# A start time for waiting streams in a kernel's written-out plan

## The chip, the core and the metric

The kernel runs on one core of a Trainium2 chip. The core has TensorE (PE; its weight loads are shown apart as PEld), VectorE (DVE), ScalarE (ACT), GpSimd (POOL) and SyncE (SP), which here only issues DMAs. Each engine works through its instructions in order, and an instruction that waits for a semaphore holds everything behind it on that engine. The metric is the device time of one execution in microseconds.

## The reference

Eight batches of 576 tokens go through two blocks. The first is causal attention with 8 heads of 64, and a bias from a running sum:

```python
s_pos = np.maximum(s, 0.0)
cum = np.cumsum(s_pos, axis=-1)
bias = -(cum[:, :, :, None] - cum[:, :, None, :])
scores = np.where(causal, -1000000000.0, scores + np.minimum(bias, 0.0))
scores = scores - np.max(scores, axis=-1, keepdims=True)
```

followed by the exponential, the division by its sum and the product with v. The second mixes the result by a two-dimensional Fourier transform over tokens and channels (its real part is added), normalizes each token, and adds a two-layer MLP of width 512 to 2048 to 512 with a relu.

## The kernel before

**Attention** goes by pairs of heads, 32 in all (`NP`). For pair i, `load` (L441) brings q and k; `high` (L491) rounds both on ScalarE into the tile KQ and puts the bias rows beside them; `low` (L517) sends copies to the tiles Q1 and K1, where VectorE (L539) and GpSimd (L532) form what the rounding left out. `maxes` (L549) computes all scores once, row-wise, to find each row's maximum: ten matmuls (L564) into three banks, each reduced by VectorE (L569, L574) into `Mx`. The maxima are transposed (L586), copied by ScalarE (L590), and sent by a DMA from ScalarE's queue into one row of KQ (L593). `scores` (L598) then computes the scores a second time, transposed, with the maxima already inside the product (L615 and L616, one bank each), and ScalarE takes the exponential into the buffer P (L621). GpSimd clears the part above the diagonal (L628, L640). `av` (L645) multiplies with the values (L676) and ScalarE copies the result into the buffers `stage` (L686, L689); `recip` (L704) and `finish` (L727) divide by the sums. KQ, Q1 and K1 have three buffers, P four (one for each head), `stage` three.

**The Fourier transform** follows for each batch when its four pairs are finished: `folds` (L771, on VectorE, GpSimd and ScalarE), then `fourier` (L825, matmuls L843 to L890 and the additions L907). Its result goes to DRAM. The conversion of the MLP's weights runs beside attention.

**The MLP** normalizes tiles of 512 tokens. The first tiles start while attention's buffers are freed one after another in `tail` (L1350); `mlp` (L1274) and `evacuate` (L1217) handle two tiles in parts, and `fast_tile` (L317) the others.

**The order of the work** up to the first fast tile is not written by hand. Each of these functions is a stream: a Python generator that yields steps, and emits instructions between them. A step names an engine, a cost in microseconds, the events it depends on, and perhaps a ring, whose next buffer must be free. `wait(...)` is a step without an engine. `Flow` (L1488) is a planner: it keeps for each engine the time at which it comes free, computes for every stream the earliest time at which its step could start, and places the earliest. Among steps of the same engine that could start within 0.05 us of it, the one with the smallest due time is placed. A placed step moves its engine's time on, and its end plus a small lag becomes an event. Due times come from the table `PR`, in which `T` is the distance of two pairs. The planned times do not go into the program; the order in which steps are placed does, for each engine by itself, since the instructions are emitted in this order. On the chip, semaphores hold each instruction until its data are there.

One property of this planner is touched by the change. When a stream passes `wait(...)`, the planner knows the event's time, but the next step of the stream, and the streams it adds, start from the time at which their engine is free and from the events they name themselves. In `scores`, the blocks' first step names no event:

```python
_, hold = yield wait(ev("row", i), ev("low", i), ring=(ring("P", 4), 3))
...
e, hold = yield pe(2 * mm(n), ring=(ring("ps", 3), 1))
```

The row's event is set in `maxes` by the step of the issue (0.74 us) and 6.5 us after it:

```python
e = yield ("ACT", 0.74, (), None)
...
e = after(e, 6.5)
```

Of the kernel before, what the change touches and what calls it, by code (L numbers as in the profile page):

```python
# [29 lines left out]
N1 = 6  # L30
NW = 8
MARGIN = 1.5
PR = {'high': -1.41, 'hstep': 1.51, 'low': -1.79, 'lstep': 1.29, 'qs': -1.97, 'mx': -0.77, 'mxh': -2.63, 'mxc': 0.92, 'mt': 9.48, 'sc': -1.53, 'sch': 7.21, 'scs': 0.71, 'sel': 9.19, 'av': 8.0, 'avh': 10.43, 'avk': 5.44, 'rc': 2.01, 'fin': 8.67, 'fold': 4.28, 'fj': 1.4, 'fst': 0.85, 'fou': 7.17, 'gap': 5.72, 'fo2': 28.57, 'fo3': 31.26, 'gap2': 0.06, 'cv': 0.11, 'T': 16.03}
BACKLOG = 4.0


# [6 lines left out]
def fused_kernel(ctx, tc, qkT, vA, sP, wP, tabD, tabS, corr, out):  # L43
# [375 lines left out]

    T = PR['T']  # L420
    L = NP - 1
# [176 lines left out]
    def scores(i):  # L598
        st = sts[i]
        qy, ky, q1, k1 = st["qy"], st["ky"], st["q1"], st["k1"]  # L600
        st["P"], st["Phold"] = [], []
        scored = Last(ev("scored", i), 12)
        for h in range(2):
            _, hold = yield wait(ev("row", i), ev("low", i), ring=(ring("P", 4), 3))
            P = attp.tile([128, PW], F32, tag="P", name="P", bufs=4)
            st["P"].append(P)
            st["Phold"].append(hold)
            diag = Last(Event(), 5)

            def one(h, c, a, n, P, diag):  # L610
                nk, q0, nq, qk = CH[c]
                ksl = slice(128 * c, 128 * c + 128)
                e, hold = yield pe(2 * mm(n), ring=(ring("ps", 3), 1))
                p = bank("ps")
                nc.tensor.matmul(p[:, :n], ky[:, h, ksl], qy[:, h, a:a + n], start=True, stop=False)  # L615
                nc.tensor.matmul(p[:, :n], k1[:, h, ksl], q1[:, h, a:a + n], start=False, stop=True)  # L616
                scored.add(e)
                lo = max(a, qk)
                o = POFF[c] + lo - qk
                e = yield act(a + n - lo, e)  # L620
                nc.scalar.activation(P[:, o:o + a + n - lo], p[:, lo - a:n], AF.Exp, scale=0.125)  # L621
                hold.add(e)
                if c < 4:
                    diag.add(e)
                else:
                    e = yield pool_(64, e)
                    d5 = P[:, POFF[4]:POFF[4] + 64]
                    nc.gpsimd.affine_select(out=d5, in_=d5, pattern=[[1, 64]], compare_op=ALU.is_ge, fill=0.0, base=0, channel_multiplier=-1)  # L628
                    ev("P5", i, h).set(e)

            x = 0
            for c, (nk, q0, nq, qk) in enumerate(CH):
                for a, n in [(0, 256), (256, 320)] if c == 0 else [(q0, nq)]:
                    flow.add(one(h, c, a, n, P, diag), T * i + PR['sc'] + PR['sch'] * h + PR['scs'] * x)
                    x += 1

            def select(P, diag, h):
                e = yield ("POOL", 0.8, (diag.event,), None)
                d4 = bass.AP(tensor=P.tensor, offset=P.offset, ap=[list(P.ap[0]), [576, 4], [1, 128]])
                nc.gpsimd.affine_select(out=d4, in_=d4, pattern=[[0, 4], [1, 128]], compare_op=ALU.is_ge, fill=0.0, base=0, channel_multiplier=-1)  # L640
                ev("P4", i, h).set(e)

            flow.add(select(P, diag, h), T * i + PR['sch'] * h + PR['sel'])

    def av(i):  # L645
        st = sts[i]
# [298 lines left out]
    def pair(i):  # L945


        yield from load(i) if i >= 3 else ()
        flow.add(high(i), T * (i + PR['high']), PR['hstep'])
        yield wait(ev("q", i, 1))  # L950
        flow.add(low(i), T * (i + PR['low']), PR['lstep'])
        flow.add(maxes(i), T * (i - 1) + PR['mt'])
        yield wait(ev("row", i), ev("low", i), *(at(("scored", i - 1)) if i else ()))
        flow.add(scores(i), T * i - 1.0)
        yield wait(ev("va", i), ev("P4", i, 0))
        flow.add(av(i), T * i + 7.0)
        yield wait(ev("sums", i))
        flow.add(recip(i), T * (i + 1) + PR['rc'])
        yield wait(ev("rb", i), *(at(("out", i - 1)) if i else ()))
        flow.add(finish(i), T * (i + 1) + PR['fin'])  # L960

    def pairs():
        for i in range(NP):
            if i >= 3:
                yield wait(ev("scored", i - 3))
            flow.add(pair(i), T * (i - 3))

    def batches():
# [248 lines left out]
    def evacuate(n, j, acc, e):  # L1217


        p, t0, f, _, _ = todo[n]  # L1220
        _, r = LN[t0]
        if p:
            e, ohold = yield ("DVE", 0.65, (e, ev("norm", t0)), (ring("oo", 2), 1))
            o = op.tile([128, TOK], F32, tag="o", name="o", bufs=2)
        else:
            e, khold = yield ("DVE", 0.65, (e, ev("norm", t0)), (ring("lt", 4), 1))
            o = lnp.tile([128, TOK], F32, tag="t", name="o", bufs=4)
        nc.vector.tensor_mul(o, r, acc[j])
        ev("acc", p, j).set(e)
        if not p:  # L1230
            got, hold = yield dma(256, *at(*(("part", last_of[1], j) for j in range(4))), ring=(ring("oo", 2), 1))
            w = op.tile([128, TOK], F32, tag="o", name="o", bufs=2)
            nc.sync.dma_start(out=w, in_=uD[j, :, t0:t0 + TOK])
            e = yield pool_(512, e, got)
            nc.gpsimd.tensor_add(o, w, o)
            hold.add(e)
            kept[j] = (o, khold)
            ev("part", n, j).set(e)
            return
        if p == 1:  # L1240
            yield wait(ev("fetched", j))
            w, hold = ws[j]
            e = yield pool_(512, e, ev("fetched", j))
            nc.gpsimd.tensor_add(w, w, o)
            ohold.add(e)
            if j == 3:
                e = yield dma(256, e)
                nc.sync.dma_start(out=uD[j, :, t0:t0 + TOK], in_=w)
                hold.add(e)
            ev("part", n, j).set(e)  # L1250
            return
        ev("rhold", t0).hold.add(e)
        yield wait(ev("part", last_of[p - 2], j))
        w, khold = kept.pop(j)
        e = yield pool_(512, e, ev("part", last_of[p - 2], j))
        nc.gpsimd.tensor_add(w, w, o)
        ohold.add(e)
        e = yield dma(256, e)
        nc.sync.dma_start(out=out[j, :, t0:t0 + TOK], in_=w)
        khold.add(e)  # L1260
        ev("part", n, j).set(e)
# [226 lines left out]
class Flow:  # L1488
# [4 lines left out]
    def __init__(self):  # L1493
        self.free = dict.fromkeys(("PE", "ACT", "DVE", "POOL", "SP"), 0.0)
        self.wire = 0.0
        self.live = []

    def add(self, gen, due, step=0.0):
        self.send([gen, due, step, None], None)

    def send(self, s, got):
        new = s[3] is None
        try:
            s[3] = s[0].send(got)
        except StopIteration:
            if not new:
                self.live.remove(s)
            return
        s[1] += s[2]
        if new:  # L1510
            self.live.append(s)

    def start(self, step):
        engine, _, deps, ring = step
        t = self.free[engine] if engine else 0.0
        if ring:
            deps = (*deps, ring[0].next())
        late = MARGIN if engine == "SP" else 0.0
        for d in deps:
            if d.t is None:  # L1520
                return None
            t = max(t, d.t + late)
        return t

    def run(self, *goals):
        while any(g.t is None for g in goals):
            ready = [(t, s) for s in self.live for t in (self.start(s[3]),) if t is not None]
            if not ready:
                raise RuntimeError("the plan is stuck: " + str([(s[0].__qualname__.split(".")[-1], s[1]) for s in self.live]))
            t, s = min(ready, key=lambda x: (x[1][3][0] is not None, x[0]))  # L1530
            engine = s[3][0]
            t, s = min(((u, v) for u, v in ready if v[3][0] == engine and u <= t + 0.05), key=lambda x: x[1][1])
            self.place(s, t)

    def place(self, s, t):
# [5 lines left out]
        elif engine:  # L1541
            self.free[engine] = t + cost
            e = Event(t + cost + self.LAG[engine])
        else:
            e = Event(t)
        self.send(s, (e, ring[0].take(ring[1])) if ring else e)

# [177 lines left out]
```

## Time and profile before

| | |
|---|---|
| time, median of 3 runs | 1433.82 us (1433.74 to 1438.87) |
| profiled execution | 1436.77 us, its span 1435.0 us |
| mean granted TensorE clock | 0.958 |
| TensorE busy | 1284.5 us, 90% of the span, 7582 matmuls |
| VectorE busy | 828.3 us, 58% |
| ScalarE busy | 632.1 us, 44% |
| GpSimd busy | 511.6 us, 36% |

Busy shares are averages over stages with different limits: attention and the Fourier transform up to about 600 us, a short change-over, then the MLP. Names like `ps<-KQ` give the tile written and a tile read, and L615 is line 615 of the kernel before. A wait is told as the instruction that waits, and the one that released it. The granted clock is the share of TensorE's full clock. Matmuls are pipelined, so that the lengths of single ones overlap.

### The profile page before, as it was taken

The numbers are of one execution on the slowest core, as the hardware profiler recorded it, in microseconds if no ns is written. First come the engines' busy times: TensorE is split into PE (matmuls) and PEld (weight loads), VectorE is DVE, ScalarE is ACT, GpSimd is POOL, SyncE is SP. The second block draws the span as 40 slices with busy tenths as digits, with TensorE's granted clock in tenths as the row PEclk, the third lists the DMA queues.
The fourth block names the chain that finished last, engine by engine and source line by source line (L and its number), as shares of the span: only waits on it lengthen the run. The fifth ranks groups of instructions, "written<-read, shape, count | busy, mean of one in ns | idle before, by whom it ended". The sixth has DMA issues, their size and how long they took to land.

```text
span 1435.0 us, 21558 instructions
## 1 busy us (share of the span) xinstructions
PE 1284.5 (90%) x7582; PEld 1129.2 (79%) x7582; DVE 828.3 (58%) x1784; ACT 632.1 (44%) x1452; POOL 511.6 (36%) x499
## 2 busy tenths in 40 slices
PE   4688777877888998889999989999999999999998
PEld 3576666766777777778878878888888888898887
DVE  5366747565766675678496568535445444554423
ACT  3566655644656565554253324333233333323321
POOL 6244446453546462573477244110211102021100
PEclk9899988978999999999999999999999999999999
DMA  8546456544545564464586233444435344342433
GB/s 219 156 120 158 121 169 183 153 125 121 155 127 157 135 173 105 128 221 142 195 257 207 98 129 103 142 138 127 167 100 177 106 147 148 125 169 89 140 125 118
DMA packets 119687, 210.79 MB, mean 147 GB/s; under 512 B 15801, under 2 KB 37753, under 8 KB 119579
## 3 DMA queue, kind: packets, MB, share of 16 engines
q1 hardware_dynamic: 116939, 206.19, 46.8%
q0 software_dynamic: 1712, 2.53, 0.8%
q8 instruction: 60, 0.98, 0.3%
q10 hardware_dynamic: 928, 0.69, 0.2%
q14 instruction: 48, 0.39, 0.1%
HBM read 153.69 MB, written 31.72 MB: 129 GB/s over the span
## 4 chain that ended last, share of the span: by engine, by line
PE 65%; DVE 12%; DMA 10%; ACT 5%; issue 4%; POOL 3%; SPq 1%; ACTq 0%; DVEq 0%; POOLq 0%
PE b L343 17%; DMA KQ<-mt 7%; PE pav L676 7%; PE acc L255 7%; PE acc L254 7%; PE acc L256 7%; PE pm L564 4%; PE ps L615 4%; PE ps L616 3%; PE h L1316 3%; PE pz L843 2%; DVE trash L574 2%; ACT P L621 1%; DVE K L539 1%; PE acc L1298 1%
## 5 line engine op out<-in xcount | busy, mean ns | idle before, releaser
L676 PE MATMUL pav<-P,va 128*128 128x320 f32 (+4 forms) x896 | 218.6, 383 | 9.2 <-ACT stage L686 3.3
L615 PE MATMUL ps<-KQ 128*128 128x256 f32 (+2 forms) x384 | 136.0, 362 | 89.3 <-DMA KQ<-mt 79.2
L676 PEld LDWEIGHTS pav<-P,va 128*128 128x128 f32 x896 | 167.0, 203 | 45.0 <-issue 8.9
L574 DVE CUSTOM_DVE_ANT_0 trash<-pm,amask 128x256 bf16<-128x256 f32 (+3 forms) x256 | 124.5, 486 | 129.8 <-PE pm L564 111.1
L621 ACT ACTIVATE P<-ps 128x320 f32<-128x320 f32 (+4 forms) x384 | 138.5, 394 | 132.0 <-PE ps L616 125.4
L255 PE MATMUL acc<-zh,w2l 128*128 128x512 f32 x452 | 179.6, 397 | 0.0
L254 PE MATMUL acc<-zh,w2h 128*128 128x512 f32 x452 | 179.2, 397 | 0.0
L256 PE MATMUL acc<-zl,w2h 128*128 128x512 f32 x452 | 177.4, 392 | 0.1
L301 POOL TENSOR_TENSOR w<-w,o 128x512 f32<-128x512 f32 x28 | 37.8, 1360 | 348.3 <-DVE o L297 309.2
L615 PEld LDWEIGHTS ps<-KQ 128*128 128x128 f32 x384 | 82.6, 215 | 100.0 <-issue 46.8
L564 PE MATMUL pm<-KQ 128*128 128x256 f32 (+3 forms) x384 | 133.3, 395 | 22.7 <-ACT KQ L509 11.8
L616 PE MATMUL ps<-Q,K 128*128 128x256 f32 (+2 forms) x384 | 125.9, 334 | 0.0
L335 ACT ACTIVATE zh<-cs 128x256 fp32r<-128x256 f32 x112 | 58.8, 525 | 142.7 <-DVE cs L355 88.5
L564 PEld LDWEIGHTS pm<-KQ 128*128 128x128 f32 x384 | 79.8, 220 | 38.4 <-DVE Mx L574 18.3
L336 DVE SCALAR_TENSOR_TENSOR zl<-cs,zh 128x256 fp32r<-128x256 f32 x112 | 66.3, 592 | 69.2 <-ACT zh L335 69.2
L343 PEld LDWEIGHTS b<-bh,wh 128*128 128x128 f32 x448 | 84.0, 188 | 25.1 <-DVE cs L355 5.7
L640 POOL TENSOR_SCALAR_AFFINE_SELECT P<-P 128x512 f32<-128x512 f32 x64 | 44.5, 695 | 160.4 <-ACT P L621 158.8
L256 PEld LDWEIGHTS acc<-zl,w2h 128*128 128x128 f32 x452 | 85.3, 189 | 19.8 <-DVE zl L336 0.6
L532 POOL TENSOR_TENSOR Q<-qk,Q 64x576 fp32r<-64x576 f32 x64 | 94.1, 1488 | 18.6 <-DMA Q<-KQ 15.0
L343 PE MATMUL b<-bh,wh 128*128 128x256 f32 x448 | 89.0, 280 | 4.4 <-DVE cs L355 4.4
L343 PE MATMUL b<-bh,wl 128*128 128x256 f32 x448 | 89.1, 280 | 0.0
L343 PE MATMUL b<-bl,wh 128*128 128x256 f32 x448 | 89.1, 280 | 0.0
(203 smaller groups left out, 2939.6 us busy)
## 6 DMA issues: line engine op xcount, KB each, us to landing
w2h<-w2D SPq DMA_DIRECT2D x128, 256.0 KB
w2l<-w2D SPq DMA_DIRECT2D x128, 256.0 KB
qk<-in_qkT_dram SPq DMA_DIRECT2D x32, 576.0 KB
raw<-in_wP_dram SPq DMA_DIRECT2D x32, 512.0 KB
va<-in_vA_dram SPq DMA_DIRECT2D x32, 480.0 KB
u<-uD SPq DMA_DIRECT2D x10, 1024.0 KB
Q<-KQ SPq DMA_DIRECT2D x32, 288.0 KB
K<-KQ SPq DMA_DIRECT2D x32, 288.0 KB
```

What stands on the lines that cost most here:

```text
L254: nc.tensor.matmul(acc[j], a[:, cs], y, start=first, stop=False)
L255: nc.tensor.matmul(acc[j], b[:, cs], y, start=False, stop=False)
L256: nc.tensor.matmul(acc[j], a[:, cs], z, start=False, stop=final)
L336: nc.vector.scalar_tensor_tensor(out=y[1][:, at], in0=src, scalar=0.0, in1=y[0][:, at].bitcast(F32), op0=ALU.max, op1=ALU.subtract)
L343: nc.tensor.matmul(p[:, 0:256], a[:, j * 128:(j + 1) * 128], b[:, j], start=start and i == 0, stop=i == 5, skip_group_check=not start)
L532: nc.gpsimd.tensor_sub(q1[64:128, h], qk[0:64, h], q1[0:64, h].bitcast(F32))
L564: nc.tensor.matmul(p[:, :n], qy[:, h, 128 * c:128 * c + 128], ky[:, h, k0:k0 + n], start=True, stop=True)
L574: nc.vector.tensor_tensor_reduce(out=trash[:, :n], in0=p[:, :n], in1=amask[:, m0:m0 + n], scale=1.0, scalar=first if x else NEG, op0=ALU.a ...
L615: nc.tensor.matmul(p[:, :n], ky[:, h, ksl], qy[:, h, a:a + n], start=True, stop=False)
L616: nc.tensor.matmul(p[:, :n], k1[:, h, ksl], q1[:, h, a:a + n], start=False, stop=True)
L621: nc.scalar.activation(P[:, o:o + a + n - lo], p[:, lo - a:n], AF.Exp, scale=0.125)
L676: nc.tensor.matmul(p[:, a - lo:n], va[:, c, vs], P[:, o:o + w], start=c == 0, stop=c == cs[-1])
```

## The change

A stream gets a fifth field, its floor. Passing a `wait` sets the floor to the time at which the wait ends in the plan; steps are placed from the floor on, and a stream that is added takes over the floor of the one that adds it. With this rule some waits would hold back streams that begin early, so they are moved: pairs begin when the scores four pairs back are done, not three; a pair no longer waits for its casts before `low` and `maxes` are added (their steps name these events themselves); and the scores of a pair follow an event "begun" of the pair before, set when its scores have been added and carrying the time of its row, in place of "scored", which is the end of its last block. In `evacuate`, a step names the event at which its pool opens. Most of the due times in `PR` change.

```diff
-PR = {'high': -1.41, 'hstep': 1.51, 'low': -1.79, 'lstep': 1.29, 'qs': -1.97, 'mx': -0.77, 'mxh': -2.63, 'mxc': 0.92, 'mt': 9.48, 'sc': -1.53, 'sch': 7.21, 'scs': 0.71, 'sel': 9.19, 'av': 8.0, 'avh': 10.43, 'avk': 5.44, 'rc': 2.01, 'fin': 8.67, 'fold': 4.28, 'fj': 1.4, 'fst': 0.85, 'fou': 7.17, 'gap': 5.72, 'fo2': 28.57, 'fo3': 31.26, 'gap2': 0.06, 'cv': 0.11, 'T': 16.03}
+PR = {'high': -1.4, 'hstep': 0.87, 'low': -1.9, 'lstep': 1.25, 'qs': -2.56, 'mx': -0.77, 'mxh': -2.85, 'mxc': 0.92, 'mt': 9.41, 'sc': -1.53, 'sch': 6.02, 'scs': 0.73, 'sel': 8.63, 'av': 9.99, 'avh': 15.59, 'avk': 4.5, 'rc': 2.01, 'fin': 26.62, 'fold': 4.29, 'fj': 1.4, 'fst': 1.56, 'fou': 7.67, 'gap': 4.39, 'fo2': 28.57, 'fo3': 32.04, 'gap2': 2.76, 'cv': 1.58, 'T': 16.07}
...
             flow.add(select(P, diag, h), T * i + PR['sch'] * h + PR['sel'])
+        ev("begun", i).set(ev("row", i))
...
         flow.add(high(i), T * (i + PR['high']), PR['hstep'])
-        yield wait(ev("q", i, 1))
         flow.add(low(i), T * (i + PR['low']), PR['lstep'])
         flow.add(maxes(i), T * (i - 1) + PR['mt'])
-        yield wait(ev("row", i), ev("low", i), *(at(("scored", i - 1)) if i else ()))
+        yield wait(ev("row", i), ev("low", i), *(at(("begun", i - 1)) if i else ()))
...
-            if i >= 3:
-                yield wait(ev("scored", i - 3))
+            if i >= 4:
+                yield wait(ev("scored", i - 4))
...
-            e, ohold = yield ("DVE", 0.65, (e, ev("norm", t0)), (ring("oo", 2), 1))
+            e, ohold = yield ("DVE", 0.65, (e, ev("norm", t0), ev("opened")), (ring("oo", 2), 1))
...
+        self.floor = 0.0
 
     def add(self, gen, due, step=0.0):
-        self.send([gen, due, step, None], None)
+        self.send([gen, due, step, None, self.floor], None)
 
     def send(self, s, got):
         new = s[3] is None
+        outer, self.floor = self.floor, s[4]
         try:
             s[3] = s[0].send(got)
...
+        finally:
+            self.floor = outer
...
-    def start(self, step):
-        engine, _, deps, ring = step
-        t = self.free[engine] if engine else 0.0
+    def start(self, s):
+        engine, _, deps, ring = s[3]
+        t = max(self.free[engine], s[4]) if engine else s[4]
...
         else:
+            s[4] = t
             e = Event(t)
```

More of the change, by code (lines that the diff above doesn't have):

```diff
@@ L1526, in run @@
         while any(g.t is None for g in goals):
-            ready = [(t, s) for s in self.live for t in (self.start(s[3]),) if t is not None]
+            ready = [(t, s) for s in self.live for t in (self.start(s),) if t is not None]
             if not ready:
```

## The prediction

> **What bounds the kernel now.** I read the page first, then busy time by stage, then the waits of TensorE in the attention stage, then its order of work around one wait, then the granted clock behind such waits.
>
> Busy time, from the first scores matmul to the last (first row), in the change-over (second) and in the MLP stage; columns: stretch, length, busy time and instructions of each engine, granted clock, DMA share, GB/s:
>
> ```profile
> 28.20:593.50 565.30, 460.35 (x2448) 396.50 (x2449) 354.06 (x997) 329.70 (x810) 270.38 (x287) 0.91 0.53 144
> ...
> 593.50:650.00 56.50, 51.37 (x320) 45.71 (x321) 42.65 (x62) 33.41 (x71) 38.02 (x32) 0.97 0.61 207
> 650.00:1435.00 785.00, 764.57 (x4799) 682.43 (x4797) 414.46 (x680) 261.48 (x561) 184.04 (x149) 0.99 0.43 142
> ```
>
> The MLP stage is TensorE's: busy 764.57 of 785.00 us at clock 0.99. The plan's rule cannot win much there: its matmul streams wait for the same events as their steps already name. Attention is different. TensorE is idle 565.30 - 460.35 = 104.95 us and its clock is 0.91, while the next busiest engine, VectorE, works 354.06 us, 63%. So nothing there is full; TensorE's in-order queue waits. What for, in the same stretch (us in total, times, longest):
>
> ```profile
> PE ps L615 <- DMA KQ<-mt: 79.2, 26, 6.4
> PE pm L564 <- DVE Mx L574: 8.0, 11, 2.2
> PE ps L615 <- DMA sums<-stage: 3.5, 1, 3.5
> PE pav L676 <- ACT stage L686: 3.3, 3, 2.9
> ```
>
> Three quarters of it, 79.2 of 104.95 us, is one wait: the scores of a pair (L615) stand for the row of maxima that ScalarE's queue sends into KQ (L593). All other causes share 25.8 us. TensorE's order at one such place (start, length, idle before and its releaser at the end):
>
> ```profile
> 435.73 0.27 PE L586 MATMUL pmt<-ident,Mx 128*10 128x128 f32 x1
> 435.76 0.36 PE L564 MATMUL pm<-KQ 128*128 128x256 f32 x1
> 435.96 1.78 PE L676 MATMUL pav<-P,va 128*128 128x320 f32 x6
> 437.34 0.53 PE L615 MATMUL ps<-KQ 128*128 128x256 f32 x1
> ...
> 437.82 0.65 PE L676 MATMUL pav<-P,va 128*128 128x192 f32 x4
> 438.28 0.54 PE L564 MATMUL pm<-KQ 128*128 128x256 f32 x2
> 442.30 0.55 PE L615 MATMUL ps<-KQ 128*128 128x256 f32 x1 [3.48 <-DMA KQ<-mt]
> ```
>
> The transpose of the maxima (L586) starts at 435.73, and the scores that need the row start at 442.30: 6.57 us. The order has only some 3.1 us of other work between them, so 3.48 us are idle. Later the same distance is filled:
>
> ```profile
> 485.58 0.27 PE L586 MATMUL pmt<-ident,Mx 128*10 128x128 f32 x1
> ...
> 490.99 0.54 PE L564 MATMUL pm<-KQ 128*128 128x256 f32 x2
> 491.36 0.28 PE L615 MATMUL ps<-KQ 128*128 128x256 f32 x1
> ```
>
> Here Fourier matmuls of another stream lie between, 5.78 us pass, and there is no wait. So the wait is one of order, not of capacity.
>
> **The change part by part.** *The floor.* In the old plan a score block's first step lists only its bank as a dependence; the wait for the row stands in the stream around it and moves nothing in time. So the plan places the block as soon as TensorE is free, though its own code counts 0.74 us for the issue and 6.5 us for the landing. With the floor, the block starts in the plan at the row's event, and TensorE's empty time before it goes to whatever is ready. Is the plan's distance right on the chip? ScalarE around the same place, and the same wait on the chain that ended last (third row: start, length):
>
> ```profile
> 436.40 0.24 ACT L590 CAST mt<-pmt 10x128 fp32r<-10x128 f32 x1
> 436.67 0.73 ACTq L593 DMA_DIRECT2D KQ<-mt  x1
> ...
> 436.67 5.50 DMA KQ<-mt
> 20.81 7.34 DMA KQ<-mt
> ```
>
> From the issue's start the row takes 5.50 us here and at most 7.34 (the startup), against 0.74 + 6.5 = 7.24 in the plan: the reserve covers it. Is there enough to fill it? TensorE's groups in the stretch (count, busy us, mean ns, idle before):
>
> ```profile
> L676 PE MATMUL pav<-P,va 128*128 128x256 f32 x864 | 210.2, 381 | 6.9 <-ACT stage L686 3.3 <-POOL P L628 1.9 <-issue 1.7
> L564 PE MATMUL pm<-KQ 128*128 128x512 f32 (+1 forms) x368 | 125.6, 386 | 9.9 <-DVE Mx L574 8.0 <-ACT KQ L513 0.4 <-issue 0.4
> ```
>
> Over 31 pairs the attention-times-values matmuls (L676) alone are 210.2 / 31 = 6.8 us a pair, with Fourier work beside them; all of pair i-1's can run while pair i's row travels. The first wait, 6.4 us at the first pair, has nothing to fill it and stays. For the others I leave half a microsecond in each of 30 pairs, 15 us, since ScalarE's queue ahead of L590 can make the row later than planned. Removed: 79.2 - 6.4 - 15 = 58 us. Bounds: 72.8 (all but the first) and 36 (half of that: fillers that are not ready either).
>
> *The clock.* Five microseconds from the end of a wait, first and last of those with a low clock, and between them one behind a short wait:
>
> ```profile
> 67.95:72.95 5.00, 5.00 (x19) 4.81 (x20) 1.89 (x7) 2.64 (x7) 0.00 (x0) 0.50 0.55 177
> ...
> 407.59:412.59 5.00, 5.00 (x18) 4.13 (x19) 1.94 (x8) 2.60 (x6) 2.34 (x2) 0.66 0.01 1
> 424.72:429.72 5.00, 5.00 (x35) 4.91 (x36) 2.18 (x13) 3.62 (x8) 1.34 (x2) 1.00 0.22 67
> ...
> 541.80:546.80 5.00, 5.00 (x17) 4.68 (x18) 2.78 (x11) 2.12 (x5) 0.42 (x1) 0.50 0.00 0
> 407.59 0.44 PE L615 MATMUL ps<-KQ 128*128 128x256 f32 x1 [2.75 <-DMA KQ<-mt]
> 424.72 0.36 PE L615 MATMUL ps<-KQ 128*128 128x256 f32 x1 [1.48 <-DMA KQ<-mt]
> ```
>
> Behind a wait of 2.75 us the clock is 0.66 and 18 matmuls run in 5 us; behind 1.48 us it is 1.00 and 35 run. Of the 17 stretches with a low clock all lie between 0.50 and 0.70; their shortfall adds up to 33 us of work at full clock (bound from the whole stretch: 460.35 x 0.09 = 41). A wait that only becomes shorter also wins this back. I take three quarters, 25 us; bounds 8 and 33.
>
> [...]
>
> *What comes instead.* The same work in a shorter stretch meets the other limits more often: VectorE's 354.06 us and ScalarE's 329.70 us would be 70% and 65% of some 505 us. The other waits, 25.8 us now, grow; I take 20 us more, bounds 0 and 26 (doubled).
>
> *Scores behind "begun" instead of "scored".* The next pair's scores need no longer follow the last of the pair before; the order of the P buffers is kept by the ring. With the floor this removes a bar that the floor would have made real. Likewise the pairs now start four back, and the wait on the casts goes: the buffers' own releases (qk, KQ) still hold the loads and casts, and every step there names its data. Taken as 0 on the path: they keep what the old plan did. Uncovered, a load later by a pair would be a new wait of the kind above, a rival below.
>
> *Other streams under the floor.* Fourier's second products and the folds, too, get their honest start; their waits on TensorE's list above are small. The change-over has only 56.50 - 51.37 = 5.1 us idle, so 0, bounds +5 and -10 (weight loads placed later while TensorE has no Fourier work left). The added dependence of the accumulator's evacuation on "opened" says only that its buffer exists: 0, covered by the MLP's first six hidden blocks.
>
> *The refitted numbers.* They set who goes first among ready steps, and cost no instruction. Two move far: the second head's values matmuls come 7.15 us later against their pair (9.99 + 15.59 after 8.00 + 10.43), which makes them the filler behind the next pairs' scores, and the finishing multiplications 18 us later (a rival). No instruction is added or removed on any engine.
>
> **Sum.** 58 + 25 - 20 = 63 us. The profiled execution took 1436.77 us (its span is 1435.0), so 1374; the median of the runs, 1433.82, is 2.95 below the profiled one: **1371 us**. Ends of the terms: 72.8 + 33 + 5 = 111 gives 1323; 36 + 8 - 26 = 18 gives 1416 (the change-over's -10 would make it 1426).
>
> **The rivals.**
>
> *The wait moves to VectorE.* With the row's wait filled by maxima blocks (L564), TensorE is three banks away from VectorE, which needs for them (rows by line, same stretch):
>
> ```profile
> L574 DVE CUSTOM_DVE_ANT_0 trash<-pm,amask 128x512 bf16<-128x512 f32 (+1 forms) x244 | 119.0, 488 | 127.1 <-PE pm L564 109.7 <-DVE Mx L574 0.5
> L574 DVE CUSTOM_DVE_ANT_0 trash<-pm,amask,M 128x320 bf16<-128x320 f32 x62 | 33.8, 545 | 21.0 <-PE pm L564 17.9 <-DVE M L569 0.2
> ```
>
> That is (119.0 + 33.8) / 31 = 4.9 us a pair against 125.6 / 31 = 4.1 us of busy matmul. For it: PE already waits for Mx 11 times. Against: VectorE itself waits 127 us for these matmuls, so it has room. Price: 45 instead of 20 us of new waits, each short enough to leave the clock alone: 58 + 25 - 45 = 38, 1396 us.
>
> *The change does not do what it says.* The old due times may already give the order that the new rule gives, and what is late on the chip is late for reasons outside the plan. For it: 7.24 us are counted correctly already. Against: the 3.1 us of filler at 435.73. Then the 79.2 us stay: 1430 us, give or take 6.
>
> *Slower: the finish holds ScalarE.* The finishing multiplications (L738, L742) free the stage buffers, three of them, that ScalarE's copies L686 and L689 write. By due times a finish lay 48.1 + 8.0 - (16.03 + 8.67) = 31.4 us ahead of the copy that reuses its buffer; now it is 48.2 + 9.99 - (16.07 + 26.62) = 15.5. If GpSimd runs later than that, the copy waits, and behind it in ScalarE's queue the exponentials, the casts and L590 with the next row: TensorE then waits for the row again. L689's waits show it once so far:
>
> ```profile
>   POOL xa L738: 4.1, 1
> ```
>
> At 4.1 us in three of five of 31 pairs it is 76 us, and the clock stays low: 58 - 76 = -18, so 1452 us; it decides from every second pair on (64 against 58). Against: GpSimd works 270.38 of 565.30 us.
>
> **How the numbers follow.** The forecast 0.58 (its own range 1323 to 1416), VectorE's wait 0.19, no effect 0.10, slower 0.13. About half a per cent, 7 us, is what a measurement of this kernel can tell from no change. Faster by more: 0.58 + 0.19, and a little of "no effect", 0.78. Within: 0.09. Slower: 0.13. For the range I leave out the lowest end, which needs every term at its best (some 0.05), and the slower case, and keep no effect: 1336 to 1436.
>
> **What would show it.** Right: the wait of L615 for the row falls from 79.2 to near 21 us; the granted clock in attention rises from 0.91 to 0.96 or more; L676 stands between L586 and the next L615; the last scores come some 60 us earlier than 593.5, and the 785 us behind them stay. The forecast is wrong if the row's wait stays over 50 us, if VectorE's Mx or ScalarE's stage takes over 40 us of TensorE, or if the change-over loses what attention wins.

## The result, and the profile after

The changed kernel takes **1363.18 us** (median of 4 runs, 1360.81 to 1364.03) beside 1435.68 for the kernel before: a ratio of **0.949, interval 0.9466 to 0.9515**. The forecast was 1371, in a range of 1336 to 1436. The profiled execution took 1363.77 us with a span of 1362.1.

The page of the kernel after, its head and the TensorE rows of the 40 slices:

```profile
span 1362.1 us, 21528 instructions
...
PE 1272.7 (93%) x7582; PEld 1112.4 (82%) x7582; DVE 831.1 (61%) x1784; ACT 625.5 (46%) x1452; POOL 511.8 (38%) x499
...
PE   5898889998989897999899899999999999999998
...
PEclk9999998999999899999999999999999999999999
```

The matmuls are the same 7582, and the other engines' busy times are within about 1% of what they were. TensorE's attention slices, mostly sevens and eights before, are now mostly eights and nines. Its busy time falls from 1284.5 to 1272.7 us for the same matmuls, while its mean granted clock rises from 0.958 to 0.975. Two stretches tell where the time went: from the first score block to the last, and from there to the end. The last score block before starts at 602.3 us; the prediction ended its stretch at 593.5, a little early. Before:

```profile
28.20:602.30 574.10, 469.15 (x2506) 404.55 (x2507) 358.71 (x1009) 335.73 (x826) 275.39 (x294) 0.91 0.52 143
```

and after, where the last two rows together are the rest (the columns are those of the prediction's first fence):

```profile
28.10:525.50 497.40, 450.52 (x2479) 380.18 (x2480) 355.87 (x994) 328.16 (x823) 278.26 (x294) 0.96 0.62 168
525.50:650.00 124.50, 114.69 (x723) 103.42 (x722) 86.87 (x127) 54.93 (x110) 63.45 (x51) 0.96 0.54 184
650.00:1362.10 712.10, 694.94 (x4357) 621.85 (x4355) 367.11 (x604) 234.84 (x510) 151.38 (x124) 0.99 0.42 139
```

The scores end after 497.40 in place of 574.10 us: 76.7 us won. The rest is 1362.1 - 525.5 = 836.6 us where it was 1435.0 - 602.3 = 832.7: 3.9 us given back. Inside the first stretch TensorE's idle time falls from 104.95 to 46.88 us (58.1 won), and its busy time from 469.15 to 450.52 (18.6 won), with the clock up from 0.91 to 0.96. Not all of the 18.6 us is shorter work: the stretch holds 27 matmuls fewer. The row ahead of it, from 0 to 28.1 us, has 12.59 us of busy TensorE in place of 8.19, and the rest has 809.63 in place of 807.14. So 4.4 us of work (8 matmuls) moved ahead and some 2.5 us (17 matmuls) behind, and 11.7 us is what the same matmuls take less over the whole kernel. What TensorE waits for in that stretch of the kernel after:

```profile
PE pm L564 <- DVE Mx L574: 26.6, 33, 3.8
PE ps L615 <- ACT P L621: 7.6, 8, 1.8
PE pz L844 <- DVE zs L852: 2.3, 1, 2.3
PE pmt L586 <- DVE Mx L574: 2.0, 3, 1.4
```

The row of maxima, 79.2 us in 26 waits before, is not in the list any more. The longest entry is now the maxima blocks' own wait for VectorE, 26.6 us in place of 8.0. In the view of the issue L593, the waits for the row that are left:

```profile
  PEld ps L615: 0.3, 1
```

And TensorE's order behind a transpose of maxima, in the kernel after:

```profile
299.82 0.28 PE L586 MATMUL pmt<-ident,Mx 128*10 128x128 f32 x1
...
300.06 0.28 PE L615 MATMUL ps<-KQ 128*128 128x256 f32 x1
...
300.88 2.92 PE L677 MATMUL pav<-P,va 128*128 128x256 f32 x14
...
309.38 3.03 PE L677 MATMUL pav<-P,va 128*128 128x256 f32 x14
...
312.83 1.36 PE L880 MATMUL py<-scos,zc 97*128 97x290 f32 x9
...
315.79 0.27 PE L586 MATMUL pmt<-ident,Mx 128*10 128x128 f32 x1
```

Between two transposes lie 16 us in which TensorE's list shows no idle time at all: score blocks of two pairs, maxima, both values products, and Fourier matmuls. The score block at 300.06 belongs to an earlier pair, for the row of this transpose is issued only at 300.42 (L593). So the row's way is filled with score blocks of earlier pairs as well as with values products.

### The profile page after: what moved, and what is told of

Read it like the earlier page. It is cut to its first block, busy times and chain, and to the rows that moved or that the text cites. A ratio compares the mean times of both kernels' runs of the same rounds, so it can differ in the third digit from the quotient of the medians.

```text
span 1362.1 us, 21528 instructions
## 1 busy us (share of the span) xinstructions
PE 1272.7 (93%) x7582; PEld 1112.4 (82%) x7582; DVE 831.1 (61%) x1784; ACT 625.5 (46%) x1452; POOL 511.8 (38%) x499
## 4 chain that ended last, share of the span: by engine, by line
PE 69%; DVE 15%; issue 5%; DMA 4%; POOL 3%; ACT 2%; SPq 1%; DVEq 0%; ACTq 0%; POOLq 0%
PE b L343 18%; PE pav L677 9%; PE acc L255 7%; PE acc L254 7%; PE acc L256 7%; PE h L1316 5%; DVE trash L574 3%; PE pm L564 3%; PE ps L615 3%; PE ps L616 2%; DVE K L539 2%; PE pz L844 2%; PE acc L1297 1%; PE acc L1298 1%; PE acc L1296 1%
## 5 line engine op out<-in xcount | busy, mean ns | idle before, releaser
L677 PE MATMUL pav<-P,va 128*128 128x320 f32 (+4 forms) x896 | 211.8, 378 | 1.1 <-POOL P L640 0.9
L677 PEld LDWEIGHTS pav<-P,va 128*128 128x128 f32 x896 | 163.5, 201 | 37.1 <-issue 6.1
L564 PE MATMUL pm<-KQ 128*128 128x256 f32 (+3 forms) x384 | 124.2, 381 | 45.6 <-DVE Mx L574 27.5
L621 ACT ACTIVATE P<-ps 128x320 f32<-128x320 f32 (+4 forms) x384 | 131.3, 394 | 47.3 <-PE ps L616 43.4
L615 PE MATMUL ps<-KQ 128*128 128x256 f32 (+2 forms) x384 | 125.9, 340 | 9.2 <-ACT P L621 7.6
L564 PEld LDWEIGHTS pm<-KQ 128*128 128x128 f32 x384 | 71.7, 200 | 71.5 <-DVE Mx L574 47.7
L616 PE MATMUL ps<-Q,K 128*128 128x256 f32 (+2 forms) x384 | 114.7, 308 | 0.0
L532 POOL TENSOR_TENSOR Q<-qk,Q 64x576 fp32r<-64x576 f32 x64 | 98.8, 1563 | 30.2 <-DMA Q<-KQ 15.2
L336 DVE SCALAR_TENSOR_TENSOR zl<-cs,zh 128x256 fp32r<-128x256 f32 x112 | 65.4, 584 | 69.3 <-ACT zh L335 69.3
L615 PEld LDWEIGHTS ps<-KQ 128*128 128x128 f32 x384 | 73.9, 192 | 17.8 <-ACT P L621 11.1
L255 PEld LDWEIGHTS acc<-zh,w2l 128*128 128x128 f32 x452 | 85.8, 190 | 2.5
```

The lines of the kernel that those rows point to most:

```text
L255: nc.tensor.matmul(acc[j], b[:, cs], y, start=False, stop=False)
L532: nc.gpsimd.tensor_sub(q1[64:128, h], qk[0:64, h], q1[0:64, h].bitcast(F32))
L564: nc.tensor.matmul(p[:, :n], qy[:, h, 128 * c:128 * c + 128], ky[:, h, k0:k0 + n], start=True, stop=True)
L677: nc.tensor.matmul(p[:, a - lo:n], va[:, c, vs], P[:, o:o + w], start=c == 0, stop=c == cs[-1])
```

## The experiments

The theory was that of the prediction: the plan put score blocks ahead of a row that it knew to be on its way, the floor stops that, and a TensorE that stands less keeps more of its clock (in the prediction's rows 0.66 behind a wait of 2.75 us, 1.00 behind one of 1.48). The rivals: the refitted due times make the gain; or the wait hides another; or the clock wins nothing. All times below are medians, ratios are against the kernel before, run beside each kernel.

**The rule with the due times of before.** The edit to the changed kernel is one line:

```diff
-PR = {'high': -1.4, 'hstep': 0.87, ... 'T': 16.07}
+PR = {'high': -1.41, 'hstep': 1.51, ... 'T': 16.03}
```

> The floor and the moved waits of the change, with the due times of before. Theory (the rule puts other work where TensorE stood for the row of maxima): the row's wait at L615 falls from 79.2 to under 15 us, the attention clock rises from 0.91 to 0.96 or more, and the time is 1375 to 1400 us. Rival (the refitted due times make the gain): the row's wait stays above 50 us or another wait of that size takes its place, 1420 us or more.

Measured: 1385.99 us, ratio 0.9663 (0.9633 to 0.9693). As the theory has it: the wait for the row is gone from the list, and the stretch of the scores is

```profile
28.40:541.30 512.90, 459.00 (x2484) 384.12 (x2485) 356.49 (x993) 328.99 (x824) 272.96 (x293) 0.94 0.59 161
```

so 61 us shorter than before; the clock, 0.94, rose less than the expected 0.96.

**The due times in the planner of before.**

```diff
-PR = {'high': -1.41, 'hstep': 1.51, ... 'T': 16.03}
+PR = {'high': -1.4, 'hstep': 0.87, ... 'T': 16.07}
```

> The refitted due times alone, in the planner of before. Theory: the plan still places score blocks ahead of their row, the row's wait stays above 50 us, and the time is 1415 to 1450 us. Rival (the due times make the gain): the row's wait is under 25 us and the time 1385 us or less.

Measured: 1438.15 us, ratio 1.0028 (1.0012 to 1.0045), with the row's wait as large as ever:

```profile
PE ps L615 <- DMA KQ<-mt: 75.5, 23, 8.7
```

The due times alone win nothing; under the rule they are worth the way from 0.9663 to 0.949, some 23 us. The first rival falls as far as it means the due times alone; of the whole gain, about a third needs them and the rule together.

**The row named at one place.** The kernel before, with the missing dependence written into the block's first step:

```diff
-e, hold = yield pe(2 * mm(n), ring=(ring("ps", 3), 1))
+e, hold = yield pe(2 * mm(n), ev("row", i), ev("low", i), ring=(ring("ps", 3), 1))
```

> The kernel before, with one edit: the first step of each score block names the events of the row and of the low parts, so that this one kind of step gets its honest start without a floor for any stream; due times of before. Theory (one missing dependence makes nearly all of it): row's wait under 15 us, 1375 to 1405 us, within 10 us of the run with the whole rule and the old due times. Rival (the floors of the other streams matter as much): 1410 us or more.

Measured: 1420.2 us, ratio 0.9901 (0.9871 to 0.9931). This is a miss for the theory. The row's wait does leave TensorE's list, but other waits come in its place:

```profile
PE pm L564 <- DVE Mx L574: 39.5, 45, 4.9
PE pmt L586 <- DVE Mx L574: 13.2, 16, 1.4
```

and the stretch of the scores keeps a low clock and much idle time, 546.10 - 474.50 = 71.6 us:

```profile
27.90:574.00 546.10, 474.50 (x2527) 393.75 (x2528) 351.42 (x1007) 330.37 (x831) 277.99 (x296) 0.92 0.56 153
```

**The score blocks exempt.** The changed kernel, with the floor taken from the score blocks:

```diff
+                    flow.floor = 0.0
                     flow.add(one(h, c, a, n, P, diag), T * i + PR['sc'] + PR['sch'] * h + PR['scs'] * x)
```

> The changed kernel, with the score blocks alone taken out of the rule: their floor is set to zero, so they are placed as soon as TensorE is free. Theory: the row's wait is back, 50 us or more, and the clock under 0.94 in attention, 1410 to 1440 us. Rival (the floors of the other streams, or the due times, carry the gain): 1390 us or less.

Measured: 1446.92 us, ratio 1.0093 (1.0063 to 1.0124), even a little above the expected range. The row's wait is back, and the stretch of the scores is the second line:

```profile
PE ps L615 <- DMA KQ<-mt: 58.0, 21, 6.4
```

```profile
28.40:584.70 556.30, 458.28 (x2479) 388.18 (x2479) 358.99 (x992) 331.20 (x817) 273.14 (x292) 0.93 0.55 148
```

All other floors together, with the new due times, shorten that stretch by 574.10 - 556.30 = 17.8 us, but the rest takes 1442.0 - 584.7 = 857.3 us in place of 832.7, so that nothing is won in the whole. Why the rest is longer was not taken apart. The floor of the score blocks is necessary for the gain, and by the run before it a bare dependence on the row is not enough.

**Which floors it takes.** Three kernels divide the run with the rule and the old due times: the floor is kept for named streams alone.

```diff
         else:
-            s[4] = t
+            if s[0].gi_code.co_name in ('scores',):
+                s[4] = t
```

> The run with the rule and the old due times (1386 us), with the floor kept for one kind of stream alone, the scores of a pair and the blocks that they add; all other streams are placed as in the kernel before; the three moved waits stay moved. Theory (with the row alone the gain was 13 us of 47; what lacked was the floor for the release of the P buffers and the moved waits, both of which are in here): 1380 to 1395 us. Rival (the floors of the Fourier streams are what lacked): 1408 to 1425 us, with more waiting of TensorE for VectorE than the full rule has.

> As the run with the floor for the scores alone, and the floor for the streams of the Fourier transform too (batches, folds, fourier and what they add); old due times. Theory (the scores' own floor and the moved waits make the gain): within 8 us of the run with the scores alone. Rival (Fourier's floors are what lacked): 15 us or more faster than that run, and within 8 us of the full rule with the old due times, 1378 to 1394 us.

> As the run with the floor for the scores alone, and the floor for the other streams of a pair too (pairs, pair, av, recip, finish and what they add), none for Fourier and the change-over; old due times. Theory: within 8 us of the run with the scores alone. Rival (Fourier's floors are what lacked): 1405 us or more. A third way, that the pair's other floors are what lacked: 1378 to 1394 us, with the scores alone 15 us or more above it.

Measured: 1395.74 us (ratio 0.9733, 0.9704 to 0.9763) for the scores alone, 1378.91 (0.9605, 0.9572 to 0.9639) with Fourier's floors, 1380.94 (0.9626, 0.9597 to 0.9655) with the pair's. The scores' own floor, with the moved waits, makes 38 of the 47 us that the whole rule makes with the old due times, 0.7 us short of the theory's range. The theory put both other runs within 8 us of the run with the scores alone and misses: each of the two groups wins 15 to 17 us on top. With Fourier's floors the rival's figures are met (1378 to 1394 us, 15 us or more faster). With the pair's floors its 1405 us are missed, and the third way (1378 to 1394 us) is met but for 0.2 us in the distance. Yet neither group can be called what lacked: either will do without the other, and the whole rule, which has both, is with 1386 us slower than either. So the floors beyond the scores' are worth something, but not a sum of parts. These four rules give different orders, which differ by up to 17 us with due times that were not fitted to them; which property of the order makes that difference stays open. What separates the run with the scores' floor from the one with the row named, 0.9733 against 0.9901, is mainly the floor for the release of P and the moved waits together. They were not separated here; under the whole rule with the new due times, the moved waits are worth 14 us (below).

**The wait without the order.** The kernel before in its old order; the row arrives early, with other data:

```diff
-        nc.sync.dma_start(out=cumD[2, 1], in_=zero)
+        nc.sync.dma_start(out=cumD[2, 1], in_=cumhl[:R, 0:S].bitcast(F32))
...
+        to = qy[2:3]... if i < NR else rowD[i]
-        nc.scalar.dma_start(out=qy[2:3]..., in_=mt.bitcast(F32))
+        nc.scalar.dma_start(out=to, in_=mt.bitcast(F32))
```

> The kernel before, its order of work unchanged; from the fourth pair on the row that the scores subtract is the running sum and comes with the bias rows, long before it is needed, and the DMA of the maxima goes to a DRAM buffer that nobody reads (so the maxima are computed and not used). Theory (the row's wait costs its 79.2 us and the cold clock behind it, some 33 us): row's wait under 15 us, clock in attention 0.96 or more, 1340 to 1375 us less 20 for new waits at most, so 1335 to 1390 us. Rival (only the wait itself counts, the clock wins nothing): clock stays near 0.91 and the time is 1375 to 1400 us. Rival (the wait hides another one behind it): 1410 us or more.

Measured: 1366.6 us, ratio 0.956 (0.9525 to 0.9595). What is left of the row's wait is that of the first three pairs (the lines of this kernel lie two lower):

```profile
PE ps L617 <- DMA KQ<-mt: 13.8, 3, 6.5
```

and the stretch of the scores takes 504.50 us at clock 0.95:

```profile
28.30:532.80 504.50, 448.57 (x2505) 381.98 (x2506) 363.38 (x1009) 333.03 (x826) 280.19 (x294) 0.95 0.59 163
```

The old order is hardly worse than the new one once the row is there in time, by 3.4 us. Its stretch is 574.10 - 504.50 = 69.6 us shorter without this one wait (all but the first three pairs'). That is the price of the wait, measured without touching the order, and it is nearly what the change wins there. It has two parts. The row's wait falls by 79.2 - 13.8 = 65.4 us, but idle time only from 104.95 to 504.50 - 448.57 = 55.93, by 49.0: other waits take back 16.4 us. Busy time falls by 20.6 us, in the same order and with the same matmuls but one. So a quarter of the wait did hide others, and the rival that the clock wins nothing is refuted.

**The clock by itself.** The kernel before, with TensorE kept at work where it waits:

```diff
                 p = bank("ps")
+                if h == c == a == 0:
+                    for _ in range(24):
+                        nc.tensor.matmul(p[:, 0:128], ones, ones, start=True, stop=True)
```

> The kernel before, with 24 matmuls of 128 columns on constants put ahead of the first score block of every pair, into the bank that this block then overwrites; they wait for nothing but the bank. Their time is added work of at most 24 x 0.11 us = 2.6 us a pair, most of it inside the wait for the row. Theory (an idle TensorE lowers its clock, and that costs some 33 us beside the wait): the clock behind the waits rises to 0.9 or more, attention to 0.96 or more, and the time falls by 10 to 30 us, to 1405 to 1425 us, though the row comes no earlier. Rival (the clock follows from something else, or the low clock costs nothing): 1436 us or more.

Measured: 1426.91 us, ratio 0.9978 (0.9961 to 0.9994): a few microseconds less at most, in an interval that ends just below 1. That is short of the theory's 1405 to 1425 us and of the rival's 1436. Its stretch of the scores, the added matmuls, and the wait that is left:

```profile
28.40:593.00 564.60, 524.25 (x3249) 465.08 (x3250) 357.74 (x1009) 333.27 (x826) 277.70 (x294) 0.96 0.53 146
```

```profile
L617 PE MATMUL ps<-ones 128*128 128x128 f32 x744 | 87.6, 274 | 0.0
```

```profile
PE ps L618 <- DMA KQ<-mt: 10.7, 6, 2.5
```

The clock is 0.96, as after the change, though the row comes no earlier. In the stretch the added matmuls take 87.6 us, 0.118 each where at most 0.11 was expected, while TensorE's idle time falls by 104.95 - (564.60 - 524.25) = 64.6. So 23 us of the added work is not paid by idle time, and still the stretch is 574.10 - 564.60 = 9.5 us shorter. The higher clock has paid for both: an estimate of some 32 us from these rows, or of 27 with the 4.4 us by which the median lies below that of the kernel beside it (1431.35). The expected gain forgot that part of the added work falls where there was no wait.

**The moved waits put back.**

```diff
+        yield wait(ev("q", i, 1))
...
-        yield wait(ev("row", i), ev("low", i), *(at(("begun", i - 1)) if i else ()))
+        yield wait(ev("row", i), ev("low", i), *(at(("scored", i - 1)) if i else ()))
...
-            if i >= 4:
-                yield wait(ev("scored", i - 4))
+            if i >= 3:
+                yield wait(ev("scored", i - 3))
```

> The changed kernel with the three moved waits put back: scores behind the end of the scores before, pairs three back, and the wait for the casts. Theory (under the floor these waits hold streams back that need not wait, so they had to move): 10 to 40 us slower than the change, 1373 to 1403 us, with more waiting at L564 for casts. Rival (each step's own events and buffers hold the streams as much anyway): within 5 us of the change, 1358 to 1368 us.

Measured: 1377.14 us, ratio 0.9637 (0.9607 to 0.9667), 14 us above the change, and the wait for the casts appears:

```profile
PE pm L564 <- ACT KQ L513: 9.8, 5, 3.9
```

As the theory has it: under the floor, a wait that used to cost nothing in the plan holds a stream back.

**The finish early.**

```diff
-'fin': 26.62
+'fin': 8.67
```

> The changed kernel with the finishing multiplications due 18 us earlier again (fin 8.67 in place of 26.62). Theory (a late finish does not hold ScalarE, GpSimd has room): within 7 us of the change, 1356 to 1370 us. Rival (the late finish holds the stage buffers and ScalarE): 10 us or more faster than the change, with fewer waits of L687 and L690 for GpSimd. A third way, that an early finish takes GpSimd from steps that TensorE needs sooner: 1375 us or more.

Measured: 1366.68 us, ratio 0.9564 (0.9534 to 0.9595), so 3.5 us above the change, within the theory's 1356 to 1370. It is not faster, and in the kernel with the late finish no copy into a stage buffer waits for GpSimd. L690, the copy that did so once before, waits for TensorE alone, and the list of the other, L687, has no GpSimd either:

```profile
L690 ACT COPY stage<-pav x64: 367/399/432, 35.2 to 534.3; 128x256 f32<-128x256 f32 x32, 128x320 f32<-128x320 f32 x32
...
  PE pav L677: 30.6, 26
  PE pm L564: 0.7, 2
```

The prediction's slower rival is refuted.

**TensorE's prices.** A try for a better version: the changed kernel with the matmul prices of the plan at what the profile shows, and one event more for the relu.

```diff
-        e, zhold = yield act(512, e, ring=(ring("z0", 3), 1))
+        e, zhold = yield act(512, e, ev("accp"), ring=(ring("z0", 3), 1))
...
-    return 0.012 + n / 2150
+    return 0.005 + n / 2330
...
-    return 0.02 + n / 537
+    return 0.01 + n / 600
```

> The changed kernel, with TensorE's prices in the plan set to what its matmuls take at full clock in the profile (320 columns of the values product 0.54 instead of 0.62 us, 256 columns of the scores 0.115 instead of 0.131), and the relu of the first tiles waiting in the plan for its pool; due times as they are. Theory (the plan gains where it says truly when a step can start; its prices are the next untruth): 5 to 15 us faster than the change, 1348 to 1358 us. Rival (the due times are fitted to the old prices, and a shorter price lets the plan place maxima that VectorE is not ready for): 1368 us or more, with more waiting at L564.

Measured: 1377.73 us, ratio 0.961 (0.9586 to 0.9633), 14.6 us slower. The theory fell. The rival's time is right but not its mechanism: the maxima blocks wait about as long as in the change.

```profile
PE pm L564 <- DVE Mx L574: 25.9, 44, 2.8
```

Truer prices, with the event for the relu and with due times fitted to the old prices, gave a poorer order. The two edits were not separated, and whether a refit would turn that round was not tried. No kernel run here beats the change.

## Why the prediction was right, point by point

It was right in the mechanism and, to 8 us, in the time; that its sum came so close owes something to errors of opposite sign. By the terms of its sum:

- **The row's wait.** Forecast 58 us of 79.2, with 72.8 as the upper bound; 77.3 were won, 72.8 inside the stretch and 4.5 ahead of it. The prediction set the 79.2 us against the 104.95 us of idle time in the stretch, but the first wait, 6.4 us, ends where the stretch begins, as a line of the kernel before shows:

```profile
28.19 0.58 PE L615 MATMUL ps<-KQ 128*128 128x256 f32 x1 [6.42 <-DMA KQ<-mt]
```

  So the row's wait is 72.8 us of the 104.95, the other causes have 32.2 and not 25.8, and all 72.8 went. Two parts of the term were wrong. The first wait was said to have nothing to fill it; in the kernel after it is filled with the second pair's maxima. The first score block starts no earlier (28.1 against 28.2 us), but work is done sooner, and idle time up to there falls from 28.20 - 8.19 = 20.0 to 28.10 - 12.59 = 15.5 us. After:

```profile
20.75 2.26 PE L564 MATMUL pm<-KQ 128*128 128x384 f32 x4 [0.35 <-ACT mt L590]
23.28 3.16 PE L564 MATMUL pm<-KQ 128*128 128x256 f32 x6 [0.26 <-DVE Mx L574]
27.69 0.38 PE L586 MATMUL pmt<-ident,Mx 128*10 128x128 f32 x1 [1.25 <-DVE Mx L574]
```

  And half a microsecond for each pair was not needed: 0.3 us of waiting for the row is left in all, so the plan's reserve covers its way. This is the term most mis-sized.
- **The clock.** Forecast 25 us; measured 11.7 us less busy time over the whole kernel. The stretch alone shows 18.6, but 6.9 of that is work that moved out of it. In the old order, with the row early, busy time fell by 20.6 us at about the same clock, and keeping TensorE at work was worth an estimated 27 to 32. So the price of the low clock was near the forecast, and the new order gives some 9 us of it back; by what, no run separates. Part of what is missing from 0.96 to 1 lies behind waits for VectorE, which took the row's place: the clock was 0.63 behind one of 3.76 us and 0.66 behind one of 2.04 (below).
- **New waits.** Forecast 20 us more of other idle time; measured 46.88 - (104.95 - 72.8) = 14.7. The rival in which VectorE takes 45 us is refuted by its size; its direction was right, the Mx wait grew from 8.0 to 26.6.
- **The change-over.** Taken as 0 with bounds +5 and -10. The time behind the last scores grew by 3.9 us, of which 2.5 is busy time, with 17 matmuls more, and 1.4 is idle time.
- **The moved waits.** Taken as 0 because they keep what the plan did; putting them back costs 14 us, so the reason holds.
- **The due times.** The prediction gave them no price of their own ("cost no instruction"). Alone they are worth nothing, under the rule 23 us. That part of the result it attributed to the floor. The rule with the old due times wins 47 us, less than the sum, and with the new ones more than the sum: that the forecast lies between is luck in part.

Together 58 + 25 - 20 = 63 became 77.3 + 11.7 - 14.7 - 1.4 = 72.9 us, the difference of the two spans. The signs it named came true: the row's wait fell (further than the 21 us named), the clock rose to 0.96, the scores end 76.7 us earlier with 3.9 us more behind them, and values products stand between a transpose and that pair's own scores. The rival without effect is refuted by the runs above.

## What to carry to other kernels

When a list scheduler writes the order of in-order queues, look for steps whose start it computes without the events that the program waits for: the largest wait in a profile, always on the same instruction, with other work ready behind it, is their mark. Here a start time that counts those events was necessary for that one kind of step, but the waits that had been harmless and the priorities had to be gone through with it, for each of them then acted differently. And price an idle TensorE with what its clock loses afterwards, not by the gap alone: here an estimated 27 to 32 us, from the run that kept it at work, beside the 79.2 us of the wait itself.

## What the runs showed of the hardware

In these traces TensorE's granted clock was low behind shorter pauses than the 2.75 us that the prediction shows, 0.66 behind one of 2.04 us, and not behind each, 1.00 behind one of 2.07 us. In the kernel after, five microseconds behind two waits for VectorE:

```profile
335.60:340.60 5.00, 5.00 (x27) 4.85 (x28) 4.35 (x12) 1.11 (x3) 0.86 (x1) 0.66 0.35 105
464.31:469.31 5.00, 3.60 (x9) 2.52 (x10) 4.67 (x15) 3.71 (x8) 1.01 (x1) 0.63 0.61 166
```

with the waits themselves:

```profile
335.60 0.92 PE L564 MATMUL pm<-KQ 128*128 128x320 f32 x2 [2.04 <-DVE Mx L574]
464.31 0.96 PE L564 MATMUL pm<-KQ 128*128 128x512 f32 x2 [3.76 <-DVE Mx L574]
```

The second stretch has another wait in it, of 1.32 us. In the first, the clock behind 2.04 us is 0.66; in the kernel before, it is 1.00 behind 2.07 us:

```profile
146.34 0.39 PE L615 MATMUL ps<-KQ 128*128 128x256 f32 x1 [2.07 <-DMA KQ<-mt]
...
146.34:151.34 5.00, 4.96 (x29) 4.42 (x30) 4.29 (x11) 4.06 (x12) 2.97 (x3) 1.00 0.73 225
```

So the length of the pause alone does not decide here; what else does was not shown.
